# Attention output with V held in 32-column tiles, the MLP cut in three, and eight PSUM banks in one pool

## The chip, the cores and the metric

The kernel runs on one core of one Trainium2 chip. The core has a matrix engine (PE, whose weight loads the profile lists apart as PEld), a vector engine (DVE), an activation engine (ACT), a general engine (POOL) and a queue engine that mainly issues DMAs (SP). Matmul results go to PSUM, eight banks of 2 KB for each of 128 partitions. The metric is the device time of one execution in microseconds (us), as the median of the runs.

## The reference

Two identical layers work on a sequence of 2048 tokens, each a vector of 576. A layer is sliding-window attention (32 heads of 18 numbers, each query sees itself and the 255 tokens before it) and then an MLP with 4608 hidden units.

```python
def _A_ref(x, wqkv, wo):                    # D = 576, H = 32, Dh = 18, W = 256
    qkv = split(x @ wqkv)                   # q, k, v by head
    scores = einsum("bhqd,bhkd->bhqk", q, k) * (Dh ** -0.5)
    mask = (q_pos - k_pos >= 0) & (q_pos - k_pos < W)
    p = softmax(where(mask, scores, -1e9))
    o = einsum("bhqk,bhkd->bhqd", p, v)
    return merge_heads(o) @ wo

def _B_ref(x, w1, b1, w2, b2):              # F = 4608
    h = gelu(layernorm(x) @ w1 + b1)
    return h @ w2 + b2

for layer in range(2):                      # the same weights in both
    x = x + _A_ref(layernorm(x), wqkv, wo)
    x = x + _B_ref(layernorm(x), w1, b1, w2, b2)
```

## The kernel before, in words

The 2048 tokens are 16 tiles of 128, and four tiles make a chunk of 512 tokens. There are eight chunks (two layers of four), and all stages go chunk by chunk; `k` is the number of the chunk.

- `qkv(k, i)` makes q, k and v of one tile: ten matmuls of 128x288 for each of the three (`two_out`, L671). DVE or ACT copies q and k from PSUM into `qn`, 32 columns per head with 18 used, and a DMA transpose puts them into `qT` and `kT`. v goes to `vA`, 20 columns per head: 18 of v and two ones, of which the first makes the sum of the softmax.
- `E(k, gs)` is attention for head groups `g` of four heads. A group's work comes in three units (two in some chunks have fewer key tiles): `scores` (L757) multiplies 32-row tiles of `qT` and `kT`, four heads at a time in four row tiles of the array; ACT takes the exponential into `pT` (L766), which has three slots; POOL writes zeros where the mask wants them (L787).
- `pv` (L804) then makes the attention output of one unit: the weights are a 128x128 piece of `pT`, what streams is 128x20 of `vA`. The result lies with queries in partitions, in one PSUM bank, `B_O`, number 7, kept for it. After the last unit DVE takes a reciprocal (L814) and multiplies (L819) into `attq`.
- `tail(k)` turns `attq` by four DMA transposes into `attT` (L848), multiplies by `wo` (L671 again, with `wo_sb`), adds to the residual `x_res` (`resid`, L838), and makes the layer norm for the MLP, turned by DMA into `xnTm`.
- `G_part(k, hf)` is the first MLP matmul and the gelu for one half of the hidden units, 18 tiles of 128: `rest` (L881) does the last 64 rows of the contraction for six hidden tiles in two 64-row tiles of the array, then four matmuls of 128x512 for each hidden tile (L893), then the gelu on ACT into `hT` (L896). ACT loads the gelu's table before a part (L938) and the exponential's after it (L936).
- `mm2(k, hf)` multiplies `hT` by that half of `w2` (L922): for each tile of tokens and each half of the 576 columns 18 matmuls of 128x288 into one bank, then `resid`.

The program's order is not written by hand. Every step is added to a list with its engine, what it reads and writes, a priority (and a correction to that by stage, `PL.nudge`) and a planned cost and latency. `Plan.schedule` lays the steps out in planned time, gives each its PSUM bank at that moment, and the engines then run their own steps strictly in that order, with semaphore waits where one step needs another. So every engine's queue is fixed before the run. Banks are in three overlapping sets: `SC` pairs (0,1), (2,3), (4,5) for scores, `FILL` (6, 5, 4) for everything that makes 288-column results, `MM1` (0 to 6) for the first MLP matmul. While chunk `k` has its attention, the MLP of chunk `k - 1` supplies PE with other work. In the first 140 us the planner also puts matmuls on a zero tile (`warm`, L579) where PE would stand idle.

## Time and profile before

| | |
|---|---|
| median of 3 runs | 928.52 us (925.98 to 930.25) |
| the profiled execution: from first to last instruction | 922.9 us |
| PE busy | 901.4 us (98%), 9411 matmuls |
| PE weight loads busy | 566.0 us (61%) |
| DVE busy | 317.0 us (34%) |
| ACT busy | 598.5 us (65%) |
| POOL busy | 365.5 us (40%) |
| granted PE clock | 1.000 |
| DMA | 128.85 MB, mean 140 GB/s |

The span of the profiled execution is 5.6 us shorter than the median of the runs; that is the part of a run outside the program's first and last instruction, together with the spread of the runs. Matmuls overlap in a pipeline and their ends are modelled, so PE's busy share says that something was in flight, not that PE ran at its rate. What PE spends on a group of matmuls is better read from the starts in the timeline: the start of the next group less the start of this one. A row of a timeline has start, length, engine, line, operation, tiles, shapes (array tile, then partitions x columns) and the count of merged instructions.

### The profile page before, as it was taken

What the parts mean: (1) busy time and instruction counts of PE and PEld (TensorE: products, weight loads), DVE (VectorE), ACT (ScalarE), POOL (GpSimd) and SP (SyncE); (2) the same over time, 40 slices, a digit from 0 to 9 for tenths busy, and PEclk for the clock granted to TensorE, in tenths of its full rate; (3) what the DMA queues carried; (4) which work ended last, traced back from release to release, by engine and by line L of the source; (5) the groups of instructions that cost most, each with busy time, mean ns of one, the idle gap of its engine ahead of it and who ended that gap; (6) DMA issues with size and microseconds to landing.
All of it is one profiled execution on the core that took longest, in us unless ns stands there. A gap on an engine that the chain in (4) does not pass through costs nothing. (4 is left out here: it accounts for less than half of the span.)

```text
span 922.9 us, 22461 instructions
## 1 busy us (share of the span) xinstructions
PE 901.4 (98%) x9411; PEld 566.0 (61%) x9411; DVE 317.0 (34%) x797; ACT 598.5 (65%) x721; POOL 365.5 (40%) x505
## 2 busy tenths in 40 slices
PE   9899899999999999999999999999999999999998
PEld 7566475665756657577565756656476565656556
DVE  5747122832335303175021713144123520241001
ACT  4887787677737777662677668656676777852541
POOL 3767353553504535061341644325442353610100
PEclk9999999999999999999999999999999999999999
DMA  7798719933395334743639451773619625174430
GB/s 196 152 228 136 202 60 232 205 124 116 63 205 143 117 116 124 185 85 80 193 64 267 61 190 41 192 174 64 200 40 214 153 72 202 43 202 152 150 116 27
DMA packets 204596, 128.85 MB, mean 140 GB/s; under 512 B 128848, under 2 KB 202448, under 8 KB 204496
## 3 DMA queue, kind: packets, MB, share of 16 engines
q1 hardware_dynamic: 199952, 120.06, 52.2%
q0 software_dynamic: 2112, 4.72, 2.0%
q10 hardware_dynamic: 2432, 2.65, 0.9%
q8 instruction: 74, 1.21, 0.5%
q14 instruction: 26, 0.21, 0.1%
HBM read 91.87 MB, written 2.36 MB: 102 GB/s over the span
## 5 line engine op out<-in xcount | busy, mean ns | idle before, releaser
L766 ACT ACTIVATE pT<-ps 128x1024 bf16<-128x1024 f32 (+2 forms) x384 | 348.8, 970 | 119.1 <-PE ps L757 117.8
L787 POOL TENSOR_SCALAR_AFFINE_SELECT pT<-pT 128x512 bf16<-128x512 bf16 (+1 forms) x368 | 281.2, 787 | 268.7 <-ACT pT L766 259.9
L922 PE MATMUL ps<-w_sb,hT 128*128 128x288 bf16 x2304 | 313.7, 286 | 1.6 <-DVE x_res L838 1.5
L896 ACT ACTIVATE hT<-ps,b1col 128x512 bf16<-128x512 f32 x288 | 197.9, 687 | 174.7 <-PE ps L893 174.7
L893 PE MATMUL ps<-xnTm,w_sb 128*128 128x512 bf16 x1152 | 260.5, 379 | 0.0
L922 PEld LDWEIGHTS ps<-w_sb,hT 128*128 128x128 bf16 x2304 | 211.8, 97 | 71.7 <-issue 17.1
L893 PEld LDWEIGHTS ps<-xnTm,w_sb 128*128 128x128 bf16 x1152 | 108.8, 98 | 138.1 <-issue 17.4
L838 DVE TENSOR_TENSOR x_res<-ps,x_res 128x288 f32<-128x288 f32 x160 | 71.3, 450 | 234.4 <-PE ps L922 212.9
L671 PE MATMUL ps<-wqkv,xnTa 128*128 128x288 bf16 x960 | 134.5, 286 | 2.7 <-DVE qn L710 1.8
L804 PEld LDWEIGHTS ps<-vA,pT 128*128 128x128 bf16 x2880 | 94.0, 96 | 25.0 <-POOL pT L787 11.6
L671 PEld LDWEIGHTS ps<-wqkv,xnTa 128*128 128x128 bf16 x960 | 86.9, 97 | 35.7 <-DVE qn L710 6.7
L804 PE MATMUL ps<-vA,pT 128*128 128x20 bf16 x2880 | 100.0, 171 | 3.5 <-POOL pT L787 2.9
L710 DVE CAST qn<-ps 128x288 bf16<-128x288 f32 x120 | 54.2, 454 | 116.8 <-PE ps L671 116.4
L904 POOL TENSOR_TENSOR x_res<-x_res,b2bc 128x576 f32<-128x576 f32 x32 | 40.8, 1275 | 115.7 <-ACT hT L896 115.6
L757 PE MATMUL ps<-qT,kT 32*128 32x384 bf16 (+2 forms) x1216 | 64.1, 276 | 4.1 <-ACT pT L766 3.0
L814 DVE RECIPROCAL rinv<-ps 128x16 f32<-128x16 f32 x64 | 16.2, 254 | 129.2 <-PE ps L804 129.0
L603 POOL TENSOR_SCALAR vtmp<-mv_all 128x1 f32<-128x1 f32 (+1 forms) x43 | 8.8, 204 | 109.0 <-DVE mv_all L594 107.5
L592 DVE BATCH_NORM_STATS2 st_all<-x_res 128x6 f32<-128x288 f32 x104 | 44.9, 448 | 12.0 <-DMA x_res<-in_A_x_dram 10.5
L671 PE MATMUL ps<-wo_sb,attT 128*128 128x288 bf16 x320 | 45.0, 286 | 1.5 <-DMA attT<-attq 0.8
L881 PE MATMUL ps<-xnTm,w_sb 64*128 64x512 bf16 x288 | 39.5, 377 | 2.5 <-DMA xnTm<-xn 1.5
L615 DVE TENSOR_SCALAR xn<-x_res,mv_all,rstd 128x576 bf16<-128x576 f32 x52 | 36.5, 705 | 14.3 <-DMA xnTm<-xn 8.6
L757 PEld LDWEIGHTS ps<-qT,kT 32*128 32x128 bf16 x1216 | 19.5, 92 | 34.6 <-issue 18.4
(43 smaller groups left out, 284.1 us busy)
## 6 DMA issues: line engine op xcount, KB each, us to landing
w_sb<-in_B_w_dram SPq DMA_DIRECT2D x48, 864.0 KB, 6.2
w_sb<-in_B_w_dram SPq DMA_DIRECT2D x48, 768.0 KB, 4.8
w_sb<-in_B_w_dram SPq DMA_DIRECT2D x96, 48.0 KB, 4.5
x_res<-in_A_x_dram POOLq DMA_DIRECT2D x4, 1152.0 KB, 7.9
out_dram<-xn SPq DMA_DIRECT2D x16, 144.0 KB, 1.8
wqkv<-in_A_wqkv_dram ACTq DMA_DIRECT2D x3, 576.0 KB, 7.4
hT<-in_A_x_dram SPq DMA_DIRECT2D x2, 576.0 KB, 4.9
wo_sb<-in_A_wo_dram ACTq DMA_DIRECT2D x1, 576.0 KB, 6.3
```

The lines of the kernel that those rows point to most:

```text
L592: add("dve", lambda e, i=i, s=s: e.bn_stats(st_all[:, t, i, :], s[:, t, i * HB:(i + 1) * HB]), reads=res, writes=[f"st{t}_{i}"], cost=0.37 ...
L671: ins = e.matmul(bank(bs[o])[:, 0:HB], lhs(c), rhs(c, o * HB), start=(c == 0), stop=(c == KD - 1))
L710: add("dve", lambda e, b=bs[o], dst=dst: e.tensor_copy(dst, bank(b)[:, 0:HB].rearrange("p (h d) -> p h d", d=DH)), reads=[bs[o]], writes=[ ...
L757: ins = e.matmul(two(bs[j // 2])[:, j % 2, col:col + nq * 128], k_of(T0 + so)[0][32 * j:32 * j + 32, g, :], qs[32 * j:32 * j + 32, g, qo * ...
L766: add("act", lambda e, h2=h2: e.activation(pT[:, sl, 2 * h2:2 * h2 + 2, lo:hi], two(bs[h2])[:, :, lo:hi], ACT.Exp, scale=SCALE), reads=[bs ...
L787: add("pool", lambda e, ap=ap, pat=pat, sgn=sgn, kind=kind: e.affine_select(ap, ap, pattern=pat, compare_op=(ALU.is_ge if kind == "d" else ...
L804: ins = e.matmul(bank(B_O)[:, o:o + VW], pT[:, sl, j, col + qi * 128:col + (qi + 1) * 128], vA[:, (T0 + so) % VS, 4 * g + j, :], start=(fi ...
L838: add("dve", lambda e: e.tensor_tensor(x_res[:, t, sl], bank(b)[:, 0:HB], x_res[:, t, sl], ALU.add), reads=[b], writes=[f"x{t}h{hh}"], cos ...
L893: ins = e.matmul(bank(bk)[:, 0:n], w1_sb[:, sl, col:col + 128], xnTm[:, k % 2, c, 0:n], start=False, stop=(c == 3))
L896: add("act", lambda e, ff=ff, fl=fl, bk=bk: e.activation(hT[:, fl, 0:n], bank(bk)[:, 0:n], ACT.Gelu_apprx_tanh, bias=b1col[:, ff:ff + 1]), ...
L904: add("pool", lambda e, t=t: e.tensor_tensor(x_res[:, t, :], x_res[:, t, :], b2bc[:, :], ALU.add), reads=["b2", f"h{fl}"], writes=X(t), co ...
L922: ins = e.matmul(bank(b)[:, 0:HB], hT[:, fl, i * 128:(i + 1) * 128], w2_sb[:, fl, hh * HB:(hh + 1) * HB], start=(fl == 0), stop=(fl == NFH ...
```

## The change

The change does six things.

1. `pv` swaps the operands: a 128x20 piece of `vA` is the weight, in a 32-column tile of the array at column 32j for the j-th head of the group, and `pT` streams, 128 to 384 columns at a time. The output lies with the head's numbers in partitions 32j to 32j+19 and queries along the bank. All units of a group are done in one step. `pT` has six slots.
2. Since the output is turned, DVE transposes its 32x32 blocks from PSUM into `oq`, takes the reciprocal and multiplies into `attq`, and transposes 32-column slices of `attq` straight into `attT`; each slice as soon as its heads are there. The four DMA transposes of `tail` go. A head group is now every eighth head, so `qn`, `wo_sb` and its loads have another order: `wo` comes in eight small DMAs of SP's queue in place of two of ACT's.
3. The MLP goes in three parts of 12 hidden tiles, with attention split 3, 3 and 2 groups around them.
4. All eight banks are in one pool: no bank is kept for `pv`, which takes one of (7, 6, 5, 4) as the 288-column results do. These four are set to zero at the start by DVE.
5. `x_in`, the first load of x, lies under `w2_sb` and not under `hT`.
6. The table of `PL.nudge` is another one.

```diff
@@ keep_warm
-        banks = [x for x in (6, 5, 4) if bank_free.get(x, 1e9) <= a]
+        banks = [x for x in (7, 6, 5, 4) if bank_free.get(x, 1e9) <= a]
@@ build_kernel
-    NFH = NF // 2
+    NPT = 3
+    NFH = NF // NPT
+    CUTS = (0, 3, 6, 8)
-    PS = 3
+    PS = 6
+    PVG = [()] * 8
+    PVLAG = 1
-    PAT = (6, 6, 6)
-    NXN = 4
+    PAT = (6, 6)
+    NXN = 3
-    PL = Plan(S, 7)
+    PL = Plan(S, 8)
-    PL.nudge = {"b": 1.83, "ea0": -1.98, "ld0+": 40.46, "eb0": 2.23, ...
+    PL.nudge = {"b": 4.11, "ld0": 32.77, "ld0+": 25.77, "eb0": -0.99, ...
-    attq = sb("attq", [P, 4, KD * 128], BF16)
+    oq = sb("oq", [P, 16, 32], FP32)
+    attq = sb("attq", [P, 16, KD * 32], BF16)
-    B_O = 7
-    FILL = (6, 5, 4)
-    MM1 = (0, 1, 2, 3, 4, 5, 6)
+    FILL = (7, 6, 5, 4)
+    OUT = (7, 6, 5, 4)
+    MM1 = (0, 1, 2, 3, 4, 5, 6, 7)
-    x_in = hT[:, :, :].rearrange("p a b -> p (a b)").rearrange("p (t d) -> p t d", d=D)
+    x_in = w2_sb
+    for i in OUT:
+        b = Bank((i,))
+        add("dve", lambda e, b=b: e.memset(bank(b), 0.0), writes=[b], cost=0.56, lat=0.1, prio=-7, alloc=[b])
@@ pv
-            for (so, qo, nq, col) in parts:
-                for qi in range(nq):
-                    for j in range(4):
-                        o = ((qo + qi) * 4 + j) * VW
-                        ins = e.matmul(bank(B_O)[:, o:o + VW], pT[:, sl, j, col + qi * 128:col + (qi + 1) * 128],
-                                       vA[:, (T0 + so) % VS, 4 * g + j, :], ...
+            todo = [(p, sl) for parts, sl in units for p in parts]
+            for n, ((so, qo, nq, col), sl) in enumerate(todo):
+                for j in range(4):
+                    ins = e.matmul(bank(bo)[32 * j:32 * j + VW, qo * 128:(qo + nq) * 128], vA[:, (T0 + so) % VS, 8 * j + g, :],
+                                   pT[:, sl, j, col:col + nq * 128], start=(first and n == 0), stop=(last and n == len(todo) - 1),
+                                   tile_position=(0, 32 * j), skip_group_check=True)
...
-            add("dve", lambda e: e.reciprocal(rinv[:, r, 0:4 * nt], O[:, :, DH]), ...
-            add("dve", lambda e: e.tensor_tensor(dst, O4, rb, ALU.mult), ...
+        add("dve", lambda e: e.transpose(oq[:, 0:4 * nt, :].rearrange("p b c -> p (b c)"), bank(bo)[:, 0:nt * 128]), ...
+        add("dve", lambda e: e.reciprocal(rinv[:, r, 0:4 * nt], oq[:, 0:4 * nt, DH]), ...
+        add("dve", lambda e: e.tensor_tensor(attq[:, 0:4 * nt, g * DH:(g + 1) * DH], oq[:, 0:4 * nt, 0:DH], rb, ALU.mult), ...
+        for c in range(KD):
+            if min((32 * c + 31) // DH, G - 1) == g:
+                add("dve", lambda e, c=c: e.transpose(attT[:, c, 0:nt * 128], attq[:, 0:4 * nt, 32 * c:32 * c + 32]), ...
@@ tail
-        for i in range(nt):
-            add("sp", lambda e, i=i: e.dma_start_transpose(attT[:, :, i * 128:(i + 1) * 128], attq[:, i, :]), ...
@@ wo_load
-        dma("act", wo_sb[:, 0:4, :], A_wo[0:512, :].rearrange("(c p) d -> p c d", p=P), ...
-        dma("act", wo_sb[0:64, 4, :], A_wo[512:576, :], ...
+        for j in range(4):
+            r = 8 * DH * j
+            dma("sp", wo_sb[32 * j:32 * j + 32, 0:4, :], A_wo[r:r + 128, :].rearrange("(c p) d -> p c d", p=32), ...
+            dma("sp", wo_sb[32 * j:32 * j + 16, 4, :], A_wo[r + 128:r + 144, :], ...
```

In the order of the program this looks as follows. The first place is PE's order in the attention of chunk 3, near the end of its head groups. Before, with L757 the scores, L922 the second MLP matmul and L804 the attention output:

```order
L757 MATMUL ps<-qT,kT 128x256 x8
L922 MATMUL ps<-w_sb,hT 128x288 x12
L804 MATMUL ps<-vA,pT 128x20 x16
L922 MATMUL ps<-w_sb,hT 128x288 x6
L757 MATMUL ps<-qT,kT 128x384 x4
L757 MATMUL ps<-qT,kT 128x128 x4
L922 MATMUL ps<-w_sb,hT 128x288 x6
L804 MATMUL ps<-vA,pT 128x20 x16
```

The same place with the change, where L776 are the scores, L947 the second MLP matmul and L821 the attention output:

```order
L776 MATMUL ps<-qT,kT 128x256 x8
L947 MATMUL ps<-w_sb,hT 128x288 x12
L776 MATMUL ps<-qT,kT 128x384 x4
L776 MATMUL ps<-qT,kT 128x128 x4
L947 MATMUL ps<-w_sb,hT 128x288 x12
L776 MATMUL ps<-qT,kT 128x384 x4
L776 MATMUL ps<-qT,kT 128x128 x4
L821 MATMUL ps<-pT,vA 20x384 x4
L821 MATMUL ps<-pT,vA 20x128 x4
L821 MATMUL ps<-pT,vA 20x384 x4
L821 MATMUL ps<-pT,vA 20x128 x4
L821 MATMUL ps<-pT,vA 20x256 x8
```

The pieces of 16 small matmuls per unit have become one block of 24 per group, which stands two units of scores behind the last scores of its group.

The second place is DVE's order for the last head groups of chunk 3. Before, with L814 the reciprocal, L819 the product, L838 `resid`, and L710 and L697 the copies of q, k and v:

```order
L838 TENSOR_TENSOR x_res<-ps,x_res 128x288 x2
L814 RECIPROCAL rinv<-ps 128x16
L819 TENSOR_TENSOR attq<-ps,rinv 128x4x72
L710 CAST qn<-ps 128x16x18 x3
L697 CAST vA<-ps 128x16x18 x2
L710 CAST qn<-ps 128x16x18 x8
L814 RECIPROCAL rinv<-ps 128x16
L819 TENSOR_TENSOR attq<-ps,rinv 128x4x72
```

With the change, L832 being the transpose from PSUM, L835 and L838 the reciprocal and the product, L842 the transpose of a slice into `attT`, and L867 what L838 was before, `resid`:

```order
L832 STREAM_TRANSPOSE oq<-ps 128x512
L867 TENSOR_TENSOR x_res<-ps,x_res 128x288
L835 RECIPROCAL rinv<-oq 128x16
L838 TENSOR_TENSOR attq<-oq,rinv 128x16x18
L867 TENSOR_TENSOR x_res<-ps,x_res 128x288 x2
L832 STREAM_TRANSPOSE oq<-ps 128x512
L867 TENSOR_TENSOR x_res<-ps,x_res 128x288
L835 RECIPROCAL rinv<-oq 128x16
L838 TENSOR_TENSOR attq<-oq,rinv 128x16x18
L842 STREAM_TRANSPOSE attT<-attq 128x512 x2
```

One transpose for each group and one for each slice have come into DVE's queue, and `resid` stands between them, the next user of PSUM banks.

The third place is the start. PE's first rows before, L579 being the matmuls on the zero tile, L629 the turning of the first normed x, L671 the first of q, k and v:

```order
L579 MATMUL ps<-warm 128x256 x35
L629 MATMUL ps<-ident,xn 128x128 x5
L579 MATMUL ps<-warm 128x256 x5
L671 MATMUL ps<-wqkv,xnTa 128x288 x10
L629 MATMUL ps<-ident,xn 128x128 x5
```

And with the change, L644, L594 and L686 being the same three:

```order
L644 MATMUL ps<-ident,xn 128x128 x5
L594 MATMUL ps<-warm 128x256 x5
L686 MATMUL ps<-wqkv,xnTa 128x288 x10
L644 MATMUL ps<-ident,xn 128x128 x5
L686 MATMUL ps<-wqkv,xnTa 128x288 x5
```

The 35 matmuls ahead of the first x are gone, since the four banks that they may use are being set to zero by DVE at that time. SP's first rows before:

```order
L536 DMA hT<-in_A_x_dram 128x576 x2
L536 DMA hT<-in_A_x_dram 128x2x576
L536 DMA w_sb<-in_B_w_dram 64x384 x6
L729 DMA_TRANSPOSE qT<-qn 128x8x128
L536 DMA hT<-in_A_x_dram 128x4x576
```

With the change:

```order
L548 DMA w_sb<-in_B_w_dram 64x384 x2
L548 DMA w_sb<-in_A_x_dram 128x576 x2
L548 DMA w_sb<-in_A_x_dram 128x2x576
L548 DMA w_sb<-in_B_w_dram 64x384 x2
L548 DMA w_sb<-in_B_w_dram 128x4x768
```

Two small loads of MLP weights now stand ahead of the first loads of x, and a large one right behind them.

More of the change, by code (lines that the diff above doesn't have):

```diff
@@ L790, in scores, with pv @@
         return sl
-    def pv(k, g, parts, sl, first, last, prio):
+    def pv(k, g, units, bo, first, last, prio):
         l, t0, nt = CH[k]
@@ new lines, in pv @@
+        rd += [f"v{(T0 + p[0]) % VS}h{o}" for parts, _ in units for p in parts for o in range(2)]
+        ncol = sum(p[2] for parts, _ in units for p in parts) * 128
+        add("pe", fn, reads=rd, writes=[bo], cost=0.19 + 0.02 * len(units) + ncol * 0.00043, prio=prio, lat=0.2,
+            alloc=([bo] if first else ()))
+        if not last:
+            return
+        add("dve", lambda e: e.transpose(oq[:, 0:4 * nt, :].rearrange("p b c -> p (b c)"), bank(bo)[:, 0:nt * 128]),
+            reads=[bo, f"aq{(g - 1) % G}"], writes=["oq"], cost=0.66, lat=0.14, prio=prio - 3)
@@ L845, in tail @@
         l, t0, nt = CH[k]
-        rd = [f"aq{g}" for g in range(G)]
-        for i in range(nt):
-            add("sp", lambda e, i=i: e.dma_start_transpose(attT[:, :, i * 128:(i + 1) * 128], attq[:, i, :]),
-                reads=rd + ["aqd"], writes=[f"aT{i}"], dma="t", ring=8, cost=1.3, lat=0.6, move=0.72, desc=640, prio=prio - 0.1)
         for i in range(nt):
```

116 lines of the change are left out of this document (62 added, 54 removed), and 22 rows, old and new, of the table add.

## The prediction

> **What bounds the kernel now.** I read the page's busy times first, then two long windows, the groups by shape, the waits, and PE's timeline for the rate of each kind of matmul. The page's head, and the engines' busy time in the first 100 us and the 800 us after them (span, then busy us by engine with the count of instructions in brackets):
>
> ```profile
> PE 901.4 (98%) x9411; PEld 566.0 (61%) x9411; DVE 317.0 (34%) x797; ACT 598.5 (65%) x721; POOL 365.5 (40%) x505
> ...
> 0.00:100.00 100.00, 89.97 (x1175) 61.95 (x1176) 62.04 (x165) 71.19 (x91) 61.93 (x101) 1.00 0.84 171
> 100.00:900.00 800.00, 791.61 (x8084) 489.20 (x8083) 251.26 (x624) 523.72 (x627) 303.53 (x404) 1.00 0.54 139
> ```
>
> PE is the bound, and no other engine is near: in the long middle PE has 8.4 us without a matmul in flight, ACT 276 us. What busy time doesn't tell is at what rate PE works. The groups by shape give the counts (last numbers: busy us, mean ns of one, idle us before them):
>
> ```profile
> L922 PE MATMUL ps<-w_sb,hT 128*128 128x288 bf16 x2304 | 313.7, 286 | 1.6 <-DVE x_res L838 1.5 <-DMA w_sb<-in_B_w_dram 0.2
> L922 PEld LDWEIGHTS ps<-w_sb,hT 128*128 128x128 bf16 x2304 | 211.8, 97 | 71.7 <-issue 17.1 <-DVE x_res L838 3.2 <-ACT pT L766 0.6
> L893 PE MATMUL ps<-xnTm,w_sb 128*128 128x512 bf16 x1152 | 260.5, 379 | 0.0
> L804 PE MATMUL ps<-vA,pT 128*128 128x20 bf16 x2880 | 100.0, 171 | 3.5 <-POOL pT L787 2.9 <-DVE attq L819 0.3
> ```
>
> And PE's timeline gives the rates, from the start of one row to the start of the next:
>
> ```profile
> 418.74 0.75 PE L804 MATMUL ps<-vA,pT 128*128 128x20 bf16 x24
> 419.35 9.35 PE L671 MATMUL ps<-wqkv,xnTa 128*128 128x288 bf16 x75
> 428.53 5.31 PE L922 MATMUL ps<-w_sb,hT 128*128 128x288 bf16 x42
> ...
> 440.75 0.82 PE L881 MATMUL ps<-xnTm,w_sb 64*128 64x512 bf16 x6
> 441.50 5.35 PE L893 MATMUL ps<-xnTm,w_sb 128*128 128x512 bf16 x24
> 446.70 0.90 PE L922 MATMUL ps<-w_sb,hT 128*128 128x288 bf16 x6
> ...
> 463.89 0.40 PE L757 MATMUL ps<-qT,kT 32*128 32x384 bf16 x8
> 464.22 0.91 PE L922 MATMUL ps<-w_sb,hT 128*128 128x288 bf16 x6
> 464.96 0.45 PE L804 MATMUL ps<-vA,pT 128*128 128x20 bf16 x12
> 465.26 1.63 PE L922 MATMUL ps<-w_sb,hT 128*128 128x288 bf16 x12
> 466.83 0.29 PE L757 MATMUL ps<-qT,kT 32*128 32x256 bf16 x4
> 467.05 1.65 PE L922 MATMUL ps<-w_sb,hT 128*128 128x288 bf16 x12
> 468.53 0.55 PE L804 MATMUL ps<-vA,pT 128*128 128x20 bf16 x16
> 469.01 0.34 PE L757 MATMUL ps<-qT,kT 32*128 32x384 bf16 x4
> 469.29 0.36 PE L804 MATMUL ps<-vA,pT 128*128 128x20 bf16 x8
> ```
>
> Read off: L804 takes 0.61 us for 24, or 25.4 ns each; L671 9.18 for 75, or 122 ns; L922 1.48 for 12 (at 467.05), or 123 ns; L893 5.20 for 24, or 217 ns; a row of L881 0.75 us. The scores, where four heads work side by side in 32-row tiles, take 0.22 us for four matmuls of 256 columns, 0.28 for four of 384, and 0.33 for 384 and 128 together: 0.05 to 0.06 us for each further 128 columns of all four, and 0.11 us that don't depend on columns. That is the price of leaving the tiled array; entering it shows at 465.26, where twelve L922 should take 1.48 and the scores start 1.57 later: 0.09 us. So a change of the array's shape costs about 0.1 us each way, and while it lasts the four tiles stream together.
>
> Summed over the program: 2304 x 0.123 + 1152 x 0.217 + 1280 of L671 (30 for q, k, v and 10 for `wo`, times 32 tiles) x 0.122 + 2880 x 0.0254 = 283 + 250 + 156 + 73 = 762 us. A full head group has 12 pieces of 128 columns, and 9 in the two chunks that begin a layer: 48 x 12 + 16 x 9 = 720 pieces. The scores are then 720 x 0.055 + 192 steps x 0.20 = 78 us, and 48 steps of L881 x 0.85 are 41. That makes 881 us; with 7.5 us until the first x is there and a few of turning at the start it is 892, and some 30 us of the 922.9 are waits. So the time is PE's issue time, and the change is to be weighed by it.
>
> **The change part by part.** *The output matmuls.* They cost 2880 x 25.4 ns = 73.2 us now. The change issues 1408 of them, in 352 sets of four, which stream the same 720 pieces if the four column tiles work together as the four row tiles do: 720 x 0.055 = 39.6 us. No row of before shows a column tile. The price lies between 720 x 0.05 = 36 us (the lower of the two rates) and the four tiles taking turns, 4 x 39.6 = 158; I take the rate of the scores, since they are the nearest row, another tiling of the same array with the same columns. The array changes its shape more often: in PE's order 478 times before and 559 times with the change (the 64 blocks often stand beside scores and share a change), 81 x 0.1 = 8.1 us, between 0 and twice that. Together 47.7 against 73.2: **-25.5 us**, with the lower rate -29. The Trainium skill, "TensorE: Matmul & The Clock Gate", table of measured speedups in Part 3, gives 2.38 for three column tiles. By an estimate from it, at 2.38/3 of full concurrency, the streaming would take 39.6/0.79 = 50 us and this term would be -15; no run here shows it yet.
>
> *The banks, slots and waits.* What stands still around the output matmuls and the engines that feed on PE:
>
> ```profile
> ACT hT L896 <- PE ps L893: 174.7, 288, 16.2
> ...
> PEld ps L804 <- POOL pT L787: 11.6, 36, 1.4
> ...
> PEld ps L671 <- DMA attT<-attq: 1.6, 2, 1.1
> ```
>
> At 36 places the weights of L804 wait for a mask, 0.32 us each. With the change there are 64 blocks in place of 192 steps, each waiting for its group's last mask, but two units of scores with mm2 matmuls stand between. With that, the bank that no group has to wait for any more, and the DMA turn that goes, I take **-2 us**; it can be -10 (all of these waits go) and the other way is a rival below. Where a block waits, everything behind it on PE waits too, since PE goes in order; the mm2 matmuls come next.
>
> *DVE and ACT.* Their prices:
>
> ```profile
> L838 DVE TENSOR_TENSOR x_res<-ps,x_res 128x288 f32<-128x288 f32 x160 | 71.3, 450 | 234.4 <-PE ps L922 212.9 <-PE ps L671 18.3 <-POOL pT L787 3.0
> L615 DVE TENSOR_SCALAR xn<-x_res,mv_all,rstd 128x576 bf16<-128x576 f32 x52 | 36.5, 705 | 14.3 <-DMA xnTm<-xn 8.6 <-POOL rstd L605 3.2 <-DVE mv_all L594 1.0
> L819 DVE TENSOR_TENSOR attq<-ps,rinv 128x288 bf16<-128x288 f32 x64 | 29.1, 455 | 2.8 <-DMA attT<-attq 1.0
> L936 ACT ACT_TABLE_LOAD x17 | 21.8, 1283 | 4.7 <-issue 4.5
> ```
>
> A third MLP part brings 64 more `resid` of 0.45 us, 28.8 us. A transpose of 512 columns isn't shown; between 288 columns at 0.45 and 576 at 0.705 it is 0.65 us, and 64 out of PSUM and 40 into `attT` make 67.6. Reciprocal and product stay. DVE goes from 317 to 413 us, 46% of the time, hidden beside PE; what shows is that a bank comes free later when several such steps queue up behind an L832 that waits for its block, and I take **+2 us** (0 to 8). If that cover fails, it is PE's next 288-column matmul that waits, for a bank. ACT gets 16 more table loads, 20.5 us, into the 174.7 us in which its gelu waits for PE: nothing. The four DMA transposes a chunk leave SP's queue, the eight loads of `wo` come into it early in chunk 0, with nothing behind them that is due at once: nothing.
>
> *The start.* PE, DVE and SP in the first microseconds:
>
> ```profile
> 1.11 6.53 PE L579 MATMUL ps<-warm 128*128 128x256 bf16 x35 [1.11 <-DVE warm L574]
> 7.47 0.44 PE L629 MATMUL ps<-ident,xn 128*128 128x128 bf16 x5
> ...
> 8.79 1.39 PE L671 MATMUL ps<-wqkv,xnTa 128*128 128x288 bf16 x10 [0.33 <-ACT xnTa L632]
> 10.01 0.44 PE L629 MATMUL ps<-ident,xn 128*128 128x128 bf16 x5
> ...
> 1.43 0.78 DVE L572 MEMSET wqkv<- 64x864 uint32 x1 [0.24 <-issue]
> 2.22 0.30 DVE L573 MEMSET wo_sb<- 64x288 uint32 x1
> 3.60 0.82 DVE L592 BATCH_NORM_STATS2 st_all<-hT 128x6 f32<-128x288 bf16 x2 [1.08 <-DMA hT<-in_A_x_dram]
> ...
> 2.19 3.88 SPq L536 DMA_DIRECT2D w_sb<-in_B_w_dram  x6
> ```
>
> Two of the small weight loads now stand ahead of x in SP's queue, 3.88/6 = 0.65 us each: x comes 1.3 us later. The four memsets of 512 columns, about 0.5 us each between 0.30 for 288 and 0.78 for 864, end near 4.6 us and hide behind that wait for x (3.60 + 1.3 = 4.9). The 35 matmuls on zeros took 6.36 us, 0.182 each, where 256 columns at the later rate (ten of 288 in 1.22 us) would take 0.109: PE ran in for 35 x 0.073 = 2.5 us, although the granted clock in the windows reads 1.00. Without them that falls on the first q, k and v. The sum is 3.8; the first matmuls also wait for x and ACT, which hides a part: **+3 us** (0 to 5).
>
> *The rest.* Three parts keep the number of L893, L881 and L922 matmuls, w1 and w2 bring the same bytes. x lies under `w2_sb` now, so the first load of w2 waits for x's last reader; behind it in SP's queue are more weights, and no matmul wants them before the first gelus are done: nothing. 922.9 - 25.5 - 2 + 2 + 3 = 900.4 us for the profiled span. The span stands 5.6 us below the median of the runs, 928.52; with that the forecast is **906.0 us**.
>
> **The rivals.** *The blocks wait for their masks.* A block needs all of its group's exponentials and masks, and if each of the 64 waits as long as the 36 places do now, 0.32 us, PE loses 20.6 us where I counted -2: span 923.0, run **928.6**, no change. For it: the last unit of a group has masks on all of its columns. Against it: 24 mm2 matmuls and two units of scores, 3.6 us, stand ahead of the block in the order. Chance 0.10.
>
> *The weights of a set are not hidden.* If the four loads of a set wait until the set before has streamed, each of 352 sets pays about 0.10 us, as four loads of the scores take in a row:
>
> ```profile
> 409.25 0.10 PEld L757 LDWEIGHTS ps<-qT,kT 32*128 32x128 bf16 x4 [0.24 <-issue]
> ...
> 413.97 0.12 PEld L757 LDWEIGHTS ps<-qT,kT 32*128 32x128 bf16 x8 [0.24 <-issue]
> ```
>
> That is +35.2 us: span 935.6, run **941**, slower. It decides from 0.06 us a set on, where 352 x 0.064 eats the 22.5 us. The Trainium skill, "TensorE: Matmul & The Clock Gate", Part 3, says that a weight load overlaps running matmuls only where the row group differs, and all column tiles use all rows; by that rule this rival would hold. Against it: L922's 2304 loads of 97 ns use all rows too and fit into a rate of 123 ns with their matmuls, and the eight loads of two sets of scores take 0.12 us, hardly more than four. Chance 0.06.
>
> *The column tiles take turns.* 158 us in place of 39.6: span 1019, run **1024**. It turns at 2.5 tiles at a time, where streaming takes the 62 us that are left after the other terms. Against it the scores' four row tiles. Chance 0.02.
>
> *More goes than PE's time.* The first 100 us have 10 us with no matmul in flight; if the blocks and the free banks let half of all 30 us of waits go, the span is 887 and the run **893** or less. Against it: with PE faster, whatever feeds it has less time. Chance 0.05, a good part of it below 891.
>
> **How the numbers follow.** The forecast's own case has 0.77: faster than 923.9, which is 0.5% below 928.52 and about what a measurement of this kernel can tell from no change. Its own range goes from 891 (streaming at the lower rate, the waits at -10, nothing lost at the start) to 914 (DVE at +8, the start at +5). The last rival on the list gives faster too, 0.82 in all; the masks give the same, 0.10; loads and turns give slower, 0.08. The range to 930 takes in the masks and leaves out loads and turns.
>
> **What the profile of after would show.** Right: a block of 24 of L821 takes about 0.85 us from its start to the next group's (12 x 0.055 + 0.2), sets within it start at the rate of their columns; PE has about 7920 matmuls, PE's issue sum falls to some 866; ACT has 49 table loads of 1283 ns, DVE about 413 us; L594's 27 matmuls, and the first L686 near 9 to 10 us with a slower rate. Wrong: L821's blocks at 1.2 us or more (loads) or 2.8 (turns); long PE waits on POOL ahead of L821, or on DVE's L832 and L867 ahead of 288-column matmuls.

## The result, and the profile after

The changed kernel takes 904.6 us (median, 902.71 to 905.94) against 927.84 us for the kernel before (925.98 to 930.25), a ratio of 0.9746 with a 95% interval of 0.9724 to 0.9767. The profiled span went from 922.9 to 901.7 us; the forecast was 900.4 for the span and 906.0 for the run. So the span came out 1.3 us above its forecast and the run 1.4 below. Between the two stood 5.6 us, which were too many: wherever a run and its own span are both on record the run is 1.7 to 2.2 us longer, and the rest of the 5.6 was spread.

The page's head and the same kind of windows as before (span, then busy us by engine with counts, granted PE clock, DMA share, GB/s):

```profile
span 901.7 us, 19658 instructions
...
PE 871.3 (97%) x7920; PEld 506.2 (56%) x7920; DVE 421.1 (47%) x969; ACT 616.5 (68%) x737; POOL 368.8 (41%) x505
...
0.00:100.00 100.00, 78.72 (x846) 48.86 (x846) 75.86 (x182) 64.40 (x84) 57.66 (x95) 0.98 0.77 162
100.00:2000.00 1900.00, 792.58 (x7075) 457.30 (x7074) 345.28 (x787) 552.06 (x654) 311.18 (x412) 1.00 0.21 56
```

PE is still the bound, with 1491 fewer matmuls and 30 us less busy time. DVE has 104 us more work and no other engine is near the span. The first 100 us are where PE stands still most: 21 us without a matmul in flight, where it was 10 (the 35 matmuls on zeros used to fill 6.5 of those). The granted clock of 0.98 there is one stretch at half clock, from 51.6 to 55.0 us, right behind a wait of PE; ten matmuls of 288 columns take 2.51 us in it and not 1.22:

```profile
51.69 2.58 PE L686 MATMUL ps<-wqkv,xnTa 128*128 128x288 bf16 x10 [2.13 <-DVE vA L716]
54.20 0.40 PE L776 MATMUL ps<-qT,kT 32*128 32x256 bf16 x4
```

PE's timeline shows the price of the new blocks, two of 24 matmuls (12 pieces of 128 columns for each head) and one of 16 (9 pieces), each between its neighbours:

```profile
296.96 0.83 PE L821 MATMUL ps<-pT,vA 128*20 128x384 bf16 x24
297.73 0.40 PE L776 MATMUL ps<-qT,kT 32*128 32x384 bf16 x8
...
311.41 0.83 PE L821 MATMUL ps<-pT,vA 128*20 128x384 bf16 x24
312.18 0.66 PE L686 MATMUL ps<-wqkv,xnTa 128*128 128x288 bf16 x4
...
410.72 0.67 PE L821 MATMUL ps<-pT,vA 128*20 128x384 bf16 x16
411.32 0.40 PE L776 MATMUL ps<-qT,kT 32*128 32x384 bf16 x8
```

From start to start a block of 24 takes 0.77 us and one of 16 takes 0.60: the three pieces between them cost 0.17, or 0.057 each, and 0.09 us don't depend on columns. All 48 blocks of 24 take 0.77 us in this trace. Before, twelve such pieces were 48 matmuls of 25.4 ns, 1.22 us.

The groups of output matmuls, their weight loads, what DVE does behind them, and the gelu's table loads on ACT (busy us, mean ns of one, idle us before them):

```profile
L821 PEld LDWEIGHTS ps<-pT,vA 128*20 128x20 bf16 x1408 | 25.6, 91 | 26.8 <-issue 14.3 <-POOL pT L806 2.1 <-POOL vtmp L618 1.4
...
L832 DVE STREAM_TRANSPOSE oq<-ps 128x512 f32<-128x512 f32 x64 | 45.7, 714 | 144.8 <-PE ps L821 144.6
L838 DVE TENSOR_TENSOR attq<-oq,rinv 128x288 bf16<-128x288 f32 x64 | 43.2, 675 | 1.8
L842 DVE STREAM_TRANSPOSE attT<-attq 128x512 bf16<-128x512 bf16 x40 | 27.3, 699 | 0.6
...
L962 ACT ACT_TABLE_LOAD x25 | 32.1, 1283 | 4.7 <-issue 4.3
L964 ACT ACT_TABLE_LOAD x24 | 30.8, 1283 | 0.4
L921 ACT ACTIVATE hT<-ps,b1col 128x512 bf16<-128x512 f32 x288 | 197.9, 687 | 188.7 <-PE ps L918 188.6
```

The gelu still waits 188.6 us for PE, more than before, so the 16 new table loads find room in that time, as forecast; no run prices them by themselves. And the waits (engine, line, what for: us, times, longest):

```profile
PE ps L686 <- DVE vA L716: 3.7, 4, 2.1
PE ps L686 <- DVE qn L729: 2.4, 4, 1.1
PEld ps L821 <- POOL pT L806: 2.1, 5, 0.7
PE ps L947 <- DMA w_sb<-in_B_w_dram: 1.4, 1, 1.4
```

The mask waits of the output matmuls went from 11.6 us at 36 places to 2.1 at 5. Among the sixteen largest waits of PE and its loads L947 stands with `w2` (1.4 us) and the gelu (1.2), no more with DVE; before, DVE's `resid` cost it 1.5 us at 5 places.

### The profile page after: what moved, and what is told of

Same layout as the page of the kernel before. It is cut to its first block, busy times and chain, and to the rows that moved or that the text cites. A ratio compares the mean times of both kernels' runs of the same rounds, so it can differ in the third digit from the quotient of the medians.

```text
span 901.7 us, 19658 instructions
## 1 busy us (share of the span) xinstructions
PE 871.3 (97%) x7920; PEld 506.2 (56%) x7920; DVE 421.1 (47%) x969; ACT 616.5 (68%) x737; POOL 368.8 (41%) x505
## 4 chain that ended last, share of the span: by engine, by line
PE 82%; DVE 5%; DMA 1%; issue 1%; POOL 1%; ACT 0%; DVEq 0%
PE ps L947 30%; PE ps L918 27%; PE ps L686 11%; PE ps L776 5%; PE ps L821 4%; PE ps L906 4%; DVE x_res L867 1%; DVE xn L630 1%; DVE st_all L607 1%; DMA w_sb<-in_B_w_dram 1%; DVE oq L832 0%; DVE xn L635 0%; POOL pT L806 0%; DVE attq L838 0%; DMA xnTm<-xn 0%
## 5 line engine op out<-in xcount | busy, mean ns | idle before, releaser
L806 POOL TENSOR_SCALAR_AFFINE_SELECT pT<-pT 128x512 bf16<-128x512 bf16 (+1 forms) x368 | 285.6, 799 | 259.4 <-ACT pT L785 255.7
L921 ACT ACTIVATE hT<-ps,b1col 128x512 bf16<-128x512 f32 x288 | 197.9, 687 | 188.7 <-PE ps L918 188.6
L947 PE MATMUL ps<-w_sb,hT 128*128 128x288 bf16 x2304 | 310.4, 287 | 1.6 <-DMA w_sb<-in_B_w_dram 1.4
L918 PE MATMUL ps<-xnTm,w_sb 128*128 128x512 bf16 x1152 | 263.2, 379 | 0.0
L947 PEld LDWEIGHTS ps<-w_sb,hT 128*128 128x128 bf16 x2304 | 213.5, 98 | 83.9 <-issue 29.7
L867 DVE TENSOR_TENSOR x_res<-ps,x_res 128x288 f32<-128x288 f32 x224 | 99.2, 447 | 206.9 <-PE ps L947 186.9
L686 PE MATMUL ps<-wqkv,xnTa 128*128 128x288 bf16 x960 | 136.5, 290 | 7.6 <-DVE vA L716 3.7
L686 PEld LDWEIGHTS ps<-wqkv,xnTa 128*128 128x128 bf16 x960 | 88.5, 99 | 46.5 <-DVE qn L729 6.4
L832 DVE STREAM_TRANSPOSE oq<-ps 128x512 f32<-128x512 f32 x64 | 45.7, 714 | 144.8 <-PE ps L821 144.6
L776 PE MATMUL ps<-qT,kT 32*128 32x384 bf16 (+2 forms) x1216 | 64.2, 276 | 0.7 <-ACT pT L785 0.5
L821 PE MATMUL ps<-pT,vA 128*20 128x384 bf16 (+2 forms) x1408 | 50.9, 277 | 1.8 <-DVE vA L716 1.2
L716 DVE CAST vA<-ps 128x288 bf16<-128x288 f32 x64 | 28.6, 449 | 34.4 <-PE ps L686 34.2
L838 DVE TENSOR_TENSOR attq<-oq,rinv 128x288 bf16<-128x288 f32 x64 | 43.2, 675 | 1.8
L686 PE MATMUL ps<-wo_sb,attT 128*128 128x288 bf16 x320 | 43.3, 286 | 0.1
L776 PEld LDWEIGHTS ps<-qT,kT 32*128 32x128 bf16 x1216 | 19.4, 92 | 42.1 <-issue 29.3
```

What stands on the lines that cost most here:

```text
L686: ins = e.matmul(bank(bs[o])[:, 0:HB], lhs(c), rhs(c, o * HB), start=(c == 0), stop=(c == KD - 1))
L776: ins = e.matmul(two(bs[j // 2])[:, j % 2, col:col + nq * 128], k_of(T0 + so)[0][32 * j:32 * j + 32, g, :], qs[32 * j:32 * j + 32, g, qo * ...
L806: add("pool", lambda e, ap=ap, pat=pat, sgn=sgn, kind=kind: e.affine_select(ap, ap, pattern=pat, compare_op=(ALU.is_ge if kind == "d" else ...
L821: ins = e.matmul(bank(bo)[32 * j:32 * j + VW, qo * 128:(qo + nq) * 128], vA[:, (T0 + so) % VS, 8 * j + g, :], pT[:, sl, j, col:col + nq * ...
L867: add("dve", lambda e: e.tensor_tensor(x_res[:, t, sl], bank(b)[:, 0:HB], x_res[:, t, sl], ALU.add), reads=[b], writes=[f"x{t}h{hh}"], cos ...
L918: ins = e.matmul(bank(bk)[:, 0:n], w1_sb[:, sl, col:col + 128], xnTm[:, k % 2, c, 0:n], start=False, stop=(c == 3))
```

## The experiments

All ratios are to the kernel before, timed beside it; its median was between 926.7 and 927.1 us in each group of runs. Spans are of the profiled execution. Where nothing else is said the edit is to the changed kernel.

### Do the column tiles work side by side? `turns`

The matmuls of a block go head by head, so that neighbours in the order use the same column tile.

```diff
-            for n, ((so, qo, nq, col), sl) in enumerate(todo):
-                for j in range(4):
+            for j in range(4):
+                for n, ((so, qo, nq, col), sl) in enumerate(todo):
```

> The changed kernel with the same output matmuls in another order inside a block: all of one head's column tile first, then the next head's, so that neighbours sit in the same tile. Theory (PE's issue time binds and the four tiles stream together in the changed kernel): a block of 12 pieces goes from 0.75 us to 48 matmul pieces of 128 columns at 0.053 us, some 2.6 us; 720 pieces x 3 x 0.053 = +115 us in all, span near 1016. Rival (the waits and the order of the program make the time, PE's streaming matters little): under +30 us. If weight loads of one tile are not hidden under its own streaming, more than +115.

Measured: 934.38 us, ratio 1.0074 (1.0050 to 1.0099), span 931.6, 29.9 us above the changed kernel. The block in PE's timeline:

```profile
306.29 1.51 PE L821 MATMUL ps<-pT,vA 128*20 128x384 bf16 x24
307.74 0.40 PE L776 MATMUL ps<-qT,kT 32*128 32x384 bf16 x8
```

A block now takes 1.45 us in place of 0.77. Forty-eight blocks x 0.68 are 33 us, about what the span shows, so nearly all of PE's time comes back and the order of the heads is worth more than the whole gain. But four tiles in turn would have made 12 pieces x 4 x 0.055 = 2.6 us, and that part of my expectation fell: even in this order nearly two tiles work at once. The single records of a block show how: starts at 0, 169, 225 and 230 ns, where the one at 230 is the second head's first matmul, although the first head's fourth, which stands ahead of it in the order, starts at 387. By these records a matmul for a free column tile does not wait for an earlier one whose tile is busy.

The 16 blocks of the chunks that begin a layer hardly suffer from the order:

```profile
425.04 0.70 PE L821 MATMUL ps<-pT,vA 128*20 128x384 bf16 x16
425.67 0.40 PE L776 MATMUL ps<-qT,kT 32*128 32x384 bf16 x8
```

They take 0.63 us where they took 0.60. A head has four matmuls there and not six, and in the records of one such block the first matmuls of all four heads start within 40 ns. So neighbours in the same tile cost time with six matmuls a head and next to none with four; what sets that limit no run shows.

### Does PE's time count one for one? `pv_twice`

Each set of four is issued twice, so that numerator and denominator of the softmax both double.

```diff
-                for j in range(4):
+                for r, j in ((0, 0), (0, 1), (0, 2), (0, 3), (1, 0), (1, 1), (1, 2), (1, 3)):
...                  # start flag only for r = 0, stop flag only for r = 1
```

> The changed kernel with each set of four output matmuls issued twice (sums and values both double, so the quotient is the same). Theory (PE binds from end to end, and one set costs its columns): 720 pieces x 0.055 = +39 us, span 941, run 943 to 945. Rival (PE waits elsewhere absorb part of it, as in the first 100 us): +20 to +30.

Measured: 939.26 us, ratio 1.0127 (1.0101 to 1.0153), span 938.3, up 36.6.

```profile
309.47 1.49 PE L821 MATMUL ps<-pT,vA 128*20 128x384 bf16 x48
310.89 0.40 PE L776 MATMUL ps<-qT,kT 32*128 32x384 bf16 x8
```

The second pass through a block costs 1.42 - 0.77 = 0.65 us, or 0.054 per piece, which is about the scores' rate; 720 x 0.054 is 39 us and 36.6 of them reach the end. This gives the streaming price without the changes of shape, and shows that added PE time reaches the end nearly one for one.

### Is DVE's new work hidden? `dve_more` and `dve_less`

`dve_more` puts one statistics instruction of 512 columns ahead of each transpose from PSUM, with the same order on all engines.

```diff
+            e.bn_stats(junk[:, g % 2, :], bank(bo)[:, 0:nt * 128])
             e.transpose(oq[:, 0:4 * nt, :]..., bank(bo)[:, 0:nt * 128])
```

> The changed kernel with one more DVE step of 512 columns out of PSUM ahead of each of the 64 transposes, some 0.65 us each, 42 us of DVE work, the program's order unchanged. Theory (DVE is hidden beside PE except in the first 100 us, where it is busy 75.9 of 100): +4 to +8 us, nearly all before 110 us. Rival (DVE sets when banks come free everywhere): +20 us or more, spread over the span. Second rival (fully hidden): within 2 us.

Measured: 917.22 us, ratio 0.9889 (0.9868 to 0.9911), span 913.7, up 12.0. Its group, and the same two windows:

```profile
L834 DVE BATCH_NORM_STATS2 junk<-ps 128x6 f32<-128x512 f32 x64 | 44.6, 697 | 144.4 <-PE ps L822 144.3
...
0.00:100.00 100.00, 78.69 (x836) 48.36 (x836) 77.02 (x190) 62.17 (x82) 55.39 (x92) 0.97 0.77 160
100.00:2000.00 1900.00, 790.85 (x7033) 457.69 (x7084) 374.72 (x844) 555.70 (x656) 315.21 (x414) 1.00 0.21 57
```

DVE's busy time rose by 30.6 us (421.1 to 451.7; the group sums to 44.6, since neighbours on DVE overlap a little), nearly all of it after the first 100 us, and 12 us, 0.39 for each, reach the end. So my theory that DVE matters in the first 100 us alone fell, and the rival of 20 us or more wasn't reached either. DVE at half load is not free cover. That it acts through the banks that are freed later is the likely way; this run doesn't isolate it.

`dve_less` makes one column of the product for each head group in place of 18; the rest of the attention output is left at zero.

```diff
-            e.tensor_tensor(attq[:, 0:4 * nt, g * DH:(g + 1) * DH], oq[:, 0:4 * nt, 0:DH], rb, ALU.mult)
+            e.tensor_tensor(attq[:, 0:4 * nt, g * DH:g * DH + 1], oq[:, 0:4 * nt, 0:1], rb, ALU.mult)
```

> The changed kernel with the 64 products of attention reduced from 16 x 18 columns to 16 x 1; the other columns of the attention output stay zero, so that part of the computation is left out. The program's order is unchanged, DVE has some 35 us less. 30.6 us more of DVE work made it 12.6 us longer. Theory (DVE's load costs in proportion, about 0.4 us for each, also in the change as it stands): 10 to 15 us less, 890 to 895. Rival (the order was planned for this load, so that only work beyond the plan is felt): 0 to 4 us less.

Measured: 899.31 us, ratio 0.9690 (0.9656 to 0.9723), span 897.0, down 4.7.

```profile
L838 DVE TENSOR_TENSOR attq<-oq,rinv 128x16 bf16<-128x16 f32 x64 | 28.1, 439 | 1.8
```

The product still takes 439 ns with 16 columns, so only 14.7 us of DVE's work went. The gain is 0.32 us for each us, near the 0.39 of the other direction, but 3.1 of the 4.7 us came early: the first MLP matmul stood at 97.5 us in place of 100.5, and x came 0.7 us sooner in that execution, which the edit doesn't explain. Without those 0.7 the price is 0.27. So by both runs DVE's work costs here some 0.3 to 0.4 of its length.

### What holds the first x up? `loads_wait`, `x_first` and `x_first_warm`

The start after, on the two DMA queues, DVE and PE:

```profile
0.80 1.21 SPq L548 DMA_DIRECT2D w_sb<-in_B_w_dram  x2
0.80 3.48 ACTq L548 DMA_DIRECT2D wqkv<-in_A_wqkv_dram  x6
2.06 1.75 SPq L548 DMA_DIRECT2D w_sb<-in_A_x_dram  x3
...
8.41 0.82 DVE L607 BATCH_NORM_STATS2 st_all<-w_sb 128x6 f32<-128x288 bf16 x2 [3.56 <-DMA w_sb<-in_A_x_dram]
...
10.93 0.71 PE L644 MATMUL ps<-ident,xn 128*128 128x128 bf16 x5 [10.93 <-DVE xn L630]
...
12.52 2.14 PE L686 MATMUL ps<-wqkv,xnTa 128*128 128x288 bf16 x10
14.49 0.44 PE L644 MATMUL ps<-ident,xn 128*128 128x128 bf16 x5
```

x is issued 1.26 us later than before (2.06 against 0.80), as forecast, but the first layer norm starts 4.8 us later (8.41 against 3.60), and PE's first matmul on x 3.46 us later (10.93 against 7.47).

`loads_wait` makes two large early loads, the second of x and a big piece of `w1`, wait for the first q of tile 2, so that they don't share the DMA engines with the first x.

```diff
-                x_load(CH[1][1], CH[1][2], ["aq3"], 0)
-                w1_load(-1, ["aq3"])
+                x_load(CH[1][1], CH[1][2], ["aq2"], 0)
+                w1_load(-1, ["aq2"])
```

(`aq3` isn't planned yet at that point, and the loads then wait for nothing.)

> The changed kernel with one edit: the second x load and the first large w1 load wait for head group 2 of chunk 0, where in the changed kernel they wait for a group that isn't in the list yet, and so start in the first 5 us beside x and the weights of q, k and v. Theory (these two loads, 1.9 MB, hold up x, whose first layer norm starts at 8.4 us against 3.6 before): the first layer norm starts at 4.5 to 5.5 us, and 2 to 4 us of the time go: run 901 to 903. Rival (the first 100 us are bound by DVE, the start doesn't matter): within 1.5 us of the changed kernel.

Measured: 916.99 us, ratio 0.9889 (0.9869 to 0.9910), span 913.0, up 11.3.

```profile
7.97 0.82 DVE L607 BATCH_NORM_STATS2 st_all<-w_sb 128x6 f32<-128x288 bf16 x2 [3.12 <-DMA w_sb<-in_A_x_dram]
```

x came 0.44 us sooner, no more, and that is within the spread: in `turns`, `pv_twice`, `dve_more` and `dve_less`, whose queues of loads are the changed kernel's, the first layer norm starts at 7.68 to 8.50 us. So the large loads aren't what holds x up: that theory fell. The time is another matter. The edit makes the planner lay out everything behind it anew, and the first MLP matmul stands at 107.9 us in place of 100.5. The two loads also come later than before, and the run doesn't part the one from the other; it warns that a new order can be worth some 10 us here.

`x_first` puts the three x loads ahead of the two small ones in SP's queue, and leaves the order as it is otherwise.

```diff
+    q = S.steps["sp"]
+    q[0:5] = q[2:5] + q[0:2]
```

> The changed kernel with one edit after the planning: in SP's queue the first three loads of x stand ahead of the two small w1 loads, as in the kernel before; all else keeps its order. The run in which the two large loads waited showed the first layer norm at 7.97 us against 8.41, so those loads are not what holds x up. Theory now: x is issued 1.3 us later than the weights of q, k and v and so queues behind their 1.9 MB; issued first it lands near 4 us, PE's first matmul comes at 6.5 to 7.5 in place of 10.9, and the time falls by 3 to 4 us, to 901. Rival (the first 100 us are paced by later loads of x, or by DVE): the first matmul is earlier but the first MLP matmul stays near 100.3 us, and the time stays within 1.5 us.

Measured: 900.0 us, ratio 0.9699 (0.9669 to 0.9730), span 898.0, down 3.7.

```profile
4.75 0.76 DVE L607 BATCH_NORM_STATS2 st_all<-w_sb 128x6 f32<-128x288 bf16 x2
...
7.59 0.71 PE L644 MATMUL ps<-ident,xn 128*128 128x128 bf16 x5 [7.59 <-POOL vtmp L618]
...
9.18 2.17 PE L686 MATMUL ps<-wqkv,xnTa 128*128 128x288 bf16 x10
11.19 0.44 PE L644 MATMUL ps<-ident,xn 128*128 128x128 bf16 x5
```

The first layer norm starts at 4.75 and waits for no DMA now: DVE's memsets end there, close to the 4.6 of the prediction. PE is 3.3 us earlier at the first q and the span 3.7 shorter, so the start counts about one for one.

`x_first_warm` adds 28 matmuls on the zero tile in front, into a bank that is being used for nothing yet.

```diff
+    S.steps["pe"].insert(0, Step("pe", lambda e: warm_fn(e, 3, 28), ...))
```

> As x_first, and 28 matmuls on the zero tile ahead of PE's first own matmul, as before the change. The changed kernel's first ten q matmuls take 0.197 us each against 0.122 before. Theory (PE runs in on real work): 1 to 2.5 us less than x_first, 899 to 900, and the first q matmuls at 0.122. Rival (x, ACT and DVE pace the first 20 us): as x_first.

Measured: 898.03 us, ratio 0.9686 (0.9655 to 0.9718), span 896.4, another 1.6 less.

```profile
1.11 5.97 PE L594 MATMUL ps<-warm 128*128 128x256 bf16 x28 [1.11 <-DVE warm L589]
...
8.61 1.39 PE L686 MATMUL ps<-wqkv,xnTa 128*128 128x288 bf16 x10 [0.33 <-ACT xnTa L647]
9.84 0.44 PE L644 MATMUL ps<-ident,xn 128*128 128x128 bf16 x5
```

The first ten q matmuls take 0.123 us each, where they took 0.197 in the changed kernel and 0.201 in `x_first`. The run-in of PE is real and 28 zero matmuls pay for it in time that is idle anyway.

It is the granted clock, although the windows read 1.00 there. The trace's record of that clock has its first entry, 1.00, at 6.3 us before the change, 14.1 in the changed kernel, 10.8 in `x_first` and 6.8 here, and a window takes the time ahead of it for 1.00. The matmuls tell: in the changed kernel the q matmuls start 0.240 us apart up to 14.1 us and 0.123 apart from then on, and before the change the zero matmuls go from 0.213 to 0.109 at 6.3 us. So PE runs at half rate for its first 3 to 6 us of work, whatever that work is.

The intervals of the two ratios overlap, so the last 1.6 us rest on the two profiles, not on the timing. PE's second group of turns comes 1.35 us earlier. The profile of `x_first` also has two stretches of 3.4 us at half clock, from 48.3 and from 96.1 us, and this one has none behind the start, so how the 1.6 divide isn't shown. This is the fastest kernel of the study, below both kernels of the comparison.

### Does one block for a group matter? `units`

The output matmuls go unit by unit, in three steps a group as before, and the order is planned anew with the same table.

```diff
-    PVG = [()] * 8
+    PVG = [(0, 1)] * 8
```

> The changed kernel with the output matmuls of a group in three steps, one for each unit, as before the change, and not in one block; the order is planned anew. PE's order then changes the array's shape 725 times, against 559. Theory (a change of shape costs 0.1 us and PE binds): +17 us, 921, with the waits as they are. Rival (shape changes are free, or the finer steps remove waits): within 5 us of the changed kernel, or below it.

Measured: 963.02 us, ratio 1.0375 (1.0339 to 1.0411), span 959.8, up 58.1. A wait of the weight loads, and one window of the kind shown above:

```profile
PEld ps L821 <- POOL pT L806: 19.3, 41, 1.6
...
800.00:900.00 100.00, 90.30 (x693) 47.43 (x692) 30.31 (x70) 57.40 (x68) 27.92 (x38) 0.91 0.39 120
```

PE's order has 725 changes of shape against 559; at 0.1 us they make the 17 us that I expected. The other 40 are in part waits: smaller steps come due sooner behind their masks (19.3 us of the loads, where the block had 2.1), and the table was fitted to another set of steps. In part they are the granted clock: 0.984 over the span, where the changed kernel has 0.998, and 0.91 in the window shown. That is 31 us at half clock in place of 4, which cost up to 14 us if PE has work all that time. The direction held, the size did not, and the run doesn't price the steps apart from the order.

### How much is the order, how much the operations? `before_plain`, `after_plain`, `pv_alone_plain`, `own_bank_plain`

Each of the two kernels has a table of corrections (`PL.nudge`) of its own. Four runs go without one: the kernel before, the changed one, the kernel before with the swap of operands and its transposes alone (halves of the MLP, the own bank, three slots, and three steps a group), and the changed one with bank 7 kept for the attention output, as before.

```diff
 all four:
+    PL.nudge = {}
 pv_alone_plain, in the kernel before: the new pv, transposes, wo_load and place of x_in, with
+    NPT = 2; PS = 3; PVG = [(0, 1)] * 8; PVLAG = 2; NXN = 3; OUT = (7,)
 own_bank_plain:
-    FILL = (7, 6, 5, 4)
-    OUT = (7, 6, 5, 4)
-    MM1 = (0, 1, 2, 3, 4, 5, 6, 7)
+    FILL = (6, 5, 4)
+    OUT = (7,)
+    MM1 = (0, 1, 2, 3, 4, 5, 6)
```

> The kernel before with an empty table of corrections to the priorities, so that the planner's order is the plain one. It shows what that table is worth: PE's matmuls are the same, shape changes 476 against 478, so what is added is waits. Both theories: 940 to 990. Beside the next two kernels it is the base of a comparison in which no order was fitted by hand.

> The changed kernel with an empty table too; 560 shape changes. Theory (the gain is PE's issue time, 24 us for the output matmuls and their shape changes, whatever the order): 15 to 30 us below before_plain. Rival (the gain comes from the new table of corrections, which fits the order better): within 8 us of before_plain, or above it.

> One part of the change alone, with an empty table: the swapped output matmuls with DVE's transposes, but the MLP in two halves, bank 7 kept for the output, three slots of pT and so three steps for each group, as before the change. 719 shape changes, and PE issues 39.6 us of output streaming + 24 us for 241 more changes against 73. Theory (PE's issue time): 5 to 12 us below before_plain, less what DVE's 70 us cost, so -10 to +5. Rival (the swap is the whole gain): 20 us or more below before_plain, like after_plain.

> after_plain (the changed kernel with an empty table, 912.3 us) with the banks as before the change: bank 7 for the output blocks alone, (6, 5, 4) for 288-column results, 0 to 6 for the first MLP matmul. 552 shape changes. It separates what pv_alone_plain left together (banks, slots and whole blocks, MLP in thirds). Theory (whole blocks make the gain, since they spare the shape changes and meet their masks once; a block needs its bank for 2 us of some 12): 0 to +6 us. Rival (the common pool makes the gain, since pv_alone_plain with its own bank was 50 us above after_plain): +20 us or more.

| without a table | median, us | ratio (95%) | span, us |
|---|---|---|---|
| `before_plain` | 947.82 | 1.0235 (1.0206 to 1.0264) | 945.1 |
| `pv_alone_plain` | 962.06 | 1.0368 (1.0329 to 1.0407) | 961.0 |
| `own_bank_plain` | 951.71 | 1.0261 (1.0231 to 1.0291) | 950.5 |
| `after_plain` | 912.31 | 0.9850 (0.9824 to 0.9875) | 909.7 |

The table is worth 20 us to the kernel before and 8 to the changed one, so the change itself gains 35.5 us in the plain orders, more than the 23 of the fitted ones. But the operand swap alone loses 14 us. The granted clock differs here too: it is 0.989 in `before_plain`, 0.986 in `pv_alone_plain` and 0.996 in the two others. What is missing from 1.000 makes up to 10, 13 and 4 us of the spans, so up to 7 of the 35.5 go with the clock. Where the time of the swap goes stand the waits of the weight loads, first of `before_plain`, then of `pv_alone_plain`:

```profile
PEld ps L799 <- POOL pT L782: 10.4, 24, 1.9
```

```profile
PEld ps L668 <- DVE qn L711: 20.0, 33, 1.8
PEld ps L803 <- POOL pT L788: 19.2, 55, 1.4
```

Masks are waited for at 55 places in place of 24, and q, k and v wait for DVE to free a bank (20.0 us; 11.1 in `before_plain`): DVE has 75 us more to do, and three banks behind it.

With six slots, whole blocks and three MLP parts this falls by 10 us (`own_bank_plain`), about what the difference in clock between these two runs could make. With one pool of banks it falls by 39 more, at the same clock. The page's line and the waits on DVE in `own_bank_plain`:

```profile
PE 894.6 (94%) x8006; PEld 513.8 (54%) x8006; DVE 424.0 (45%) x966; ACT 613.3 (65%) x737; POOL 364.9 (38%) x505
...
PEld ps L759 <- ACT pT L768: 38.1, 96, 1.4
PEld ps L930 <- DVE x_res L850: 19.9, 36, 1.4
PE ps L930 <- DVE x_res L850: 10.4, 24, 1.1
```

and the scores' wait in `after_plain`:

```profile
PEld ps L759 <- ACT pT L768: 13.2, 42, 1.4
```

L930, the second MLP matmul, is PE's spare work. It waits for `resid` at 24 places, for a bank to write to, since `resid` is what empties one; in `after_plain` no such wait stands among the sixteen largest on PE and its loads. As I read it, PE comes to the scores too early where the spare work can't run, and those wait for ACT 96 times in place of 42. The kept bank alone doesn't make these waits: in `pv_alone_plain`, with the same three banks but the MLP in halves, the loads of this matmul wait for `resid` 2.3 us, and in `before_plain` 0.8. They come with the thirds, where a bank is full after 12 matmuls and not 18; the pool with halves wasn't run. The pool's two parts, the fourth bank for results of 288 columns and the eighth for the first MLP matmul, weren't run apart either. Every one of these runs also has a new order, which was worth some 10 us in `loads_wait` and up to 20 in the tables; 39 is beyond these, though not beyond what `units` lost with a table that didn't fit its steps. My expectation of 0 to 6 fell and its rival held.

## Why the prediction was right, point by point

**PE is the bound: shown.** `pv_twice` puts 39 us on PE and 36.6 come out at the end; `turns` puts 33 on it and 29.9 come out. To split the two spans I went through the starts of the PE records and put each interval down to its matmul's rate or, beyond that, to waiting: 887.6 + 30.7 us before, 862.0 + 25.3 after, with the first matmul at 10.9 in place of 1.1 (the rest of both spans lies behind the last one). So issue gives 25.6, waits give 5.4, and the later first matmul takes 9.8 back. In the 25.6 are some 2 us of zero matmuls, of which there are 27 in place of 46; what is left is near the term for the output matmuls.

**Output matmuls, -25.5: right.** Forty-eight blocks x (0.77 + 0.09) + 16 x (0.60 + 0.09) make 52.3, where the second number is the change into a block, and the 47 changes that a block shares with scores beside it take 4.7 back: 47.6, against the forecast's 47.7. The streaming price of 0.055 was the scores'; the blocks give 0.057 and `pv_twice` 0.054. The estimate by the Trainium skill, "TensorE: Matmul & The Clock Gate", Part 3, from its speedup for three column tiles, gave -15 for this term; the trace doesn't agree, the four tiles stream side by side at the scores' rate.

**Weights of a set not hidden, 941: wrong, as weighed.** The loads take 91 ns each, four of them 0.36 us if they stood in line, and the sets of a block still start 0.055 us apart for each 128 columns. The rule of the Trainium skill, "TensorE: Matmul & The Clock Gate", Part 3, that a load overlaps running matmuls only across row groups would have given this rival; the trace doesn't agree. All loads of these blocks use all rows, and in one block the second set's four start 12 to 22 ns after the first matmuls, which stream until 168 ns.

**Turns, 1024: wrong.** `turns` shows what the order of heads is worth, 30 us, and that even with the heads one after another a block takes 1.45 us, not 2.6.

**Blocks wait for their masks, 928.6: wrong.** 2.1 us at 5 places, not 20.6 at 64. `units` points to the block as the reason: with three steps a group the same waits are 19.3, though in another order.

**Banks, slots and waits, -2: the sum is right, its reading is not.** Waits on PE fell by 5.4 us in the records, DVE's part in them included, so nothing in the two fitted kernels contradicts -2. But I took the pool for a small gain on top. In the plain orders it is what lets the gain out at all: without it the change stands at 950.5 (span), 5 us above `before_plain`. The step that failed is the one that priced the pool by the waits of the kernel before. My reading of why those were small, which no run shows by itself, is that the kernel's own order had been made around its banks, that its MLP came in halves, and that its DVE had a quarter less to do.

**DVE +2: about right, by two misses.** DVE came to 421 us, not 413. The product, which I said stays, went from 455 to 675 ns now that it reads `oq` and writes `attq` in another layout (which of the two costs it wasn't tried), 14 us more; the transposes took 0.714 and 0.699, not 0.65, or 73.0 us in place of 67.6. (The groups of after sum to more than 421, since neighbours overlap.) And cover at 46% of the time is no cover that costs nothing: `dve_more` and `dve_less` price DVE's work at 0.3 to 0.4 of its length. By that the 104 us that were added would cost 31 to 42, about what the common pool is worth in the plain orders. My reading, which no run shows by itself, is that two large terms meet here where my sum had +2 and -2.

**The start, +3: nearly right, with another mechanism.** PE's first matmul on x came 3.46 us later, the five turns and five zero matmuls up to the first q took 0.27 longer, and the ten cold q matmuls cost 0.075 x 10 = 0.75: 4.5 us, inside the 0 to 5. I had x 1.3 us late and 2.5 us of run-in. It was 4.8 us late, of which 1.35 was hidden, since the way from the first layer norm to PE's first matmul took 2.52 us in place of 3.87. The run-in cost 1.0 and not 2.5, because the half rate lasted 3.1 us from PE's first matmul on and not 5.2 as before the change. And the prediction took the 1.00 of the windows for the clock at the start; the matmuls' own rate shows half of it. `x_first` returned 3.7 us and `x_first_warm` 1.6.

**Sum.** The span's difference is -21.2. With -25.6 for the output matmuls and 4.5 for the start, -0.1 is left for everything else, where the forecast had -2 and +2; that is a remainder and no measurement, with the 1.3 us of the half clock at 52 us inside it, which the forecast had no term for. That the total of -22.5 came so close owes something to luck: the start came out 1.5 higher, and two terms that are far from settled cancel as they did in the forecast.

**Open.** What the kept bank would cost with a table fitted to it wasn't run. Slots, whole blocks and MLP thirds are worth 10 us together in the plain orders, not separated, and that is no more than a new order or the lower clock can be worth. The pool without the thirds wasn't run. Why x lands 4.8 us late when issued 1.26 us late isn't settled: without the large loads it still starts at 7.97, the six loads of `wqkv` in ACT's queue and the two small ones ahead of it are left.

## What to carry to other kernels

Weigh a matmul by its issue time between neighbours in the timeline, and where a 128x20 piece streams, see whether the 20 can be the weight in a column tile with three others beside it, with the heads in the innermost loop. Before trusting such a gain, ask which banks the engine that empties PSUM will hold longer, and give the spare matmul work every bank; a kernel whose order was fitted to its banks may hide what they cost. Where a window shows waits of PE, read its granted clock beside them. And look at the first rows of each DMA queue: here a swap of five issues returned a sixth of the whole gain.
